# A new order list for every engine and for the transfer queue of a gated linear attention with an MLP behind it

## The chip, the cores and the metric

The kernel runs on one core of a Trainium2 chip. That core has a matrix engine (TensorE, PE in the profile, with its weight loads as PEld), a vector engine (VectorE, DVE), a scalar engine (ScalarE, ACT), a general engine (GpSimd, POOL), a sequencer that only issues transfers here (SyncE, SP), and 16 DMA engines that carry the transfers. The metric is the device time of one execution in microseconds, as the median of several executions; lower is better.

## The reference

Four batches of eight heads with 768 steps and a head width of 48 go through a gated linear attention, and its output (3072 tokens of 384 features) through a two-layer MLP with a leaky ReLU.

```
f = 1 / (1 + exp(-f_logit))
for t in range(S):
    state = f[:, :, t, :, None] * state + outer(k[:, :, t], v[:, :, t])
    y[:, :, t] = q[:, :, t] @ state
...
h = x @ w_in                      # 3072 x 384 by 384 x 2048
g = max(0.01 * h, h)
out = g @ w_out                   # 2048 x 384
```

## The kernel before

The recurrence is computed in chunks of 128 steps: decayed scores inside a chunk, a state carried between chunks. The work is cut into 12 units of 256 tokens. Units 0 to 3 are one batch each, with its first two chunks ("paired"); units 4 to 11 are one later chunk (c = 2 to 5) of two batches. Every unit goes through the same steps. The code keeps a function for each step, and the words below are the keys of the table `parts`:

- `Lf`, `Lk`, `Lq`, `Lv`: loads of the gate logits, k, q and v, all issued by SP (L161 for paired units, L165 for the others). The number at the end is the half (0 or 1), or 2 for both halves at once.
- `ge`, `gl`: exp and ln on ACT, giving the log of the gate; `cs`: its cumulative sum by matmuls on PE (L232 to L243); `dec`: exp of the sums on ACT.
- `k`, `q`: k and q times the decays (L263), on DVE (last number 0) or on POOL (last number 1); `v`: v to bf16 on POOL (L268 and after).
- the turning of k and q: for paired units on PE (`tk`, `tq`, L296) with copies out (`ck`, `cq`), for the others by a transposing DMA on SP's queue (`xk`, `xq`, L316).
- `sc`: scores on PE (L332, L339); `mk`: their mask on DVE (L349, L353); `mx`, `ms`: scores times v and the carried state (L370); `xt`: the result as the MLP's input; `pt`, `sf`, `sb`: the update of the state (PE L435 and L440, DVE, POOL).
- `up`: one of 8 groups of the first layer, 6 matmuls of 256 columns (L468); `pr`: leaky ReLU on ACT (L473); `dn`: a quarter of the second layer for 128 tokens, 4 matmuls of 384 columns (L480); `dh`: half of the columns of the last 128 tokens, all 16 matmuls (L496); `ob`, `st`: copy out of PSUM and store (L515 on SP).
- `WI`, `WO`: the weights in four blocks each, loaded by SP in fp32 (L170, L174) into the last two raw buffers, and turned to bf16 (`CI`, `CO`) in thirds on DVE, ACT or POOL.
- `F`: fills, matmuls of 512 columns on constant data whose result nobody reads; the number is their count.

Nothing is scheduled by the compiler. One string, `order`, lists all steps, with the engine where there is a choice, and after `@` the PSUM banks. The program walks this string and emits each step, so each engine's queue holds its steps in the string's order, SP's loads, transposes and stores among them. Every engine works through its own queue strictly in order and waits where data or a buffer is not ready.

```
    for word in order.split():
        word, _, at = word.partition("@")
        name, *numbers = word.split("_")
        parts[name](*[int(n) for n in numbers], *[int(n) for n in at.split(".") if n])
```

Buffers also set the order: six raw buffers for f and k and six for q and v (unit j uses number j modulo 6), three buffers for scaled k and q, two for the turned ones, three for the MLP's input and inner layer, four output tiles, eight PSUM banks.

Of the kernel before, what the change touches and what calls it, by code (L numbers as in the profile page):

```python
# [15 lines left out]
def kernel(  # L16
# [134 lines left out]
    def raw(j, x):  # L151
        return (raw_fk if x in "fk" else raw_qv)[j % NB][:, "fkqv".index(x) % 2]

    def by_pair(t):
        return t.rearrange("t a h d -> t (a h d)").rearrange("t (h s d) -> t h s d", s=2, d=D)

    def load(x):
        def go(j, a):
            if paired(j):
                h = slice(0, H) if a == 2 else slice(4 * a, 4 * a + 4)  # L160
                nc.sync.dma_start(out=by_pair(raw(j, x))[:, h].rearrange("t h s d -> t h (s d)"),  # L161
                                  in_=srcs[x][j, h, 0:2 * C, :].rearrange("h (t s) d -> t h (s d)", s=2))
            else:
                c, h = units[j]
                nc.sync.dma_start(out=raw(j, x)[:, a],  # L165
                                  in_=srcs[x][2 * h + a, :, c * C:(c + 1) * C, :].rearrange("h t d -> t h d"))
        return go
# [368 lines left out]
    pt_1_2@4.6 dec_0_0 k_0_0_1 ck_1_0_0 F_2@0 sc_1_0@5.7 ge_2_1 ge_2_0 q_0_0_1 sf_1_0 sc_0_1@0.3 mk_1_0_1 gl_2_1
    tk_0_0@2 mk_1_0_0 sb_1_0 F_1@4 cs_2_1@1 tq_0_0@4 mx_1_2@7.5 gl_2_0 ge_3_1 ck_0_0_0 v_0_0 cs_2_0@2 ge_3_0 gl_3_1
    dec_2_1 v_0_1 cq_0_0_0 mk_0_1_0 mk_0_1_1 xt_1_0_0 ms_1 zs_0_1 pt_0_2@4.0 sc_0_0@1.3 xt_1_1_1 gl_3_0 CI_3_2_1
    CI_3_0_2 sf_0_0 sb_0_0 CI_3_1_0 mk_0_0_1 cs_3_1@5 dec_3_1 dec_2_0 cs_3_0@7 k_2_0_1 mk_0_0_0 up_1_7@4 up_1_6@5
    q_2_0_1 pr_1_7 mx_0_2@3.1 pr_1_6 k_2_1_0 zv_2_1 q_2_1_0 ms_0 tk_2_0@2 tq_2_1@4 xt_0_1_1 xt_0_0_0 cq_2_1_0 sf_0_1  # L540
    dec_3_0 tk_2_1@5 ck_2_0_0 tq_2_0@3 CI_0_2_2 ck_2_1_0 CI_0_0_2 up_0_6@1 up_0_7@4 sf_1_1 v_2_0 cq_2_0_1 sc_2_0@7.0
    sc_2_1@3.2 v_2_1 mk_2_0_1 mk_2_1_1 mk_2_1_0 mk_2_0_0 CI_0_1_1 pr_0_7 up_0_0@5 up_1_1@4 CI_1_2_2 up_0_1@6 pr_0_1
    up_1_0@0 pt_2_2@2.3 pr_1_1 CI_1_1_1 mx_2_2@7.6 CI_1_0_0 pr_0_0 sf_2_0 q_3_0_0 xt_2_0_1 up_0_2@4 up_0_3@5 pr_1_0
    sb_2_0 ms_2 zs_3_0 k_3_0_0 sf_2_1 WO_0 CI_2_1_2 q_3_1_1 k_3_1_0 xt_2_1_1 up_1_2@2 up_1_3@7 CI_2_0_1 up_2_2@0
    up_2_7@6 WO_1 pr_0_2 CI_2_2_1 pr_2_2 pr_1_2 pr_0_6 pr_0_3 pr_1_3 up_2_5@4 up_0_4@0 WO_2 up_1_4@2 tq_3_1@1 pr_0_4
# [10 lines left out]
    cs_6_0@7 up_3_7@1 dn_2_0_1 dec_6_0 sb_2_1 k_5_2_1 q_5_2_0 up_3_6@0 xk_5 xq_5 Lv_4_1 v_5_2 Lk_6_0 Lq_6_0 ob_1_1_1
    st_1_1 Lq_6_1 dn_3_1_0@6 Lf_9_1 st_0_0 dn_3_1_1 gl_7_2 pr_3_7 pr_3_5 dn_3_0_1 sc_4_1@7.4 mk_4_1_0 pr_3_6
    sc_4_0@1.2 Lv_6_0 dn_3_0_2 Lf_8_0 v_4_2 dn_3_0_3 dn_3_1_2 dn_3_1_3 sc_5_0@0.7 mk_4_0_1 ob_3_0_1 mk_4_0_0 mk_4_1_1
    sc_5_1@2.1 pt_5_0@3 dn_2_0_2 cs_7_0@4 mk_5_0_1 mk_5_1_0 mk_5_1_1 dn_2_0_3 pt_4_1@7 mx_5_1@2 mk_5_0_0 sf_5_0
    dec_7_0 xt_5_1_1 mx_5_0@1 mx_4_1@4 mx_4_0@0 cs_6_1@3 xt_5_0_1 ob_3_1_1 dec_6_1 pt_4_0@2 up_5_3@1 up_5_4@6  # L560
    xt_4_1_1 up_5_5@3 Lf_8_1 Lf_9_0 sb_5_0 q_6_2_0 sf_4_1 Lq_8_1 xt_4_0_0 pr_5_5 pr_5_4 Lv_7_1 Lk_7_0 sb_4_1 up_5_6@4
    cs_7_1@7 k_6_2_0 Lk_7_1 sf_4_0 ob_2_0_0 dec_7_1 up_5_7@3 up_5_2@0 pr_5_6 sb_4_0 k_7_2_1 q_7_2_0 up_5_0@6 up_5_1@7
    pr_5_3 up_4_2@4 pr_5_0 up_4_6@2 up_4_1@1 up_4_4@5 pt_5_1@6 pr_5_1 up_4_0@7 xk_6 sf_5_1 pr_4_1 Lv_7_0 Lv_6_1 xq_6
    pr_5_7 up_4_7@1 pr_4_2 xk_7 v_7_2 pr_5_2 sb_5_1 xq_7 pr_4_0 ge_8_2 up_4_3@3 up_4_5@4 Lf_10_1 dn_5_0_0@6 pr_4_4
    dn_5_0_1 Lf_10_0 st_2_0 st_3_0 gl_8_2 pr_4_3 cs_8_0@0 pr_4_5 pr_4_7 pt_7_0@7 dn_4_0_0@5 dn_4_0_1 sf_7_0 pr_4_6
# [62 lines left out]
```

## Time and profile before

| | |
|---|---|
| three executions | 181.9, 183.21, 185.36 us; median 183.21 us |
| profiled execution | 180.78 us, of which the span from first to last instruction is 179.0 us |
| granted TensorE clock | 1.0 |
| busy in the span | PE 94%, PEld 73%, ACT 60%, DVE 46%, POOL 40% |
| DMA | 34.44 MB, mean 192 GB/s |

The profile is of one execution. "Idle before" is the time in which an engine stood still ahead of an instruction, with what ended that wait behind the arrow. In a timeline, a row merges equal instructions in a run; its first column is the start in microseconds, its second how long they took together, and a wait is shown in brackets. The chain of waits follows the last instruction back, from each step to what released it.

### The profile page before, as it was taken

The page shows a single profiled execution, that of the slowest core. Times are in us where ns is not written, and L with a number is a line of the kernel's source. Part 1 is how long each engine was busy: PE and PEld are TensorE (multiplying, and loading weights), DVE is VectorE, ACT ScalarE, POOL GpSimd, SP SyncE. Part 2 cuts the span into 40 slices and gives each one's busy share as a digit, 9 for nine tenths or more (in the row PEclk, how much of TensorE's full clock was granted, in tenths as well). Part 3 has the DMA queues.
Part 4 walks back from the last instruction along what each step waited for, and adds up shares of the span by engine and source line. Part 5 has one row for each costly group of instructions (what it writes and reads, how often), then busy time and mean ns, then how long its engine had stood idle before and what let it go on. Part 6 is the DMA issues. An engine that isn't in the chain of part 4 may idle for free.

```text
span 179.0 us, 5543 instructions
## 1 busy us (share of the span) xinstructions
PE 167.6 (94%) x2302; PEld 131.0 (73%) x2302; DVE 82.5 (46%) x172; ACT 108.1 (60%) x234; POOL 72.3 (40%) x143
## 2 busy tenths in 40 slices
...
GB/s 149 302 319 346 299 355 291 270 405 275 189 221 188 205 231 190 236 167 218 153 190 267 201 193 211 231 155 249 210 169 245 2 4 0 48 44 0 88 4 176
DMA packets 105961, 34.44 MB, mean 192 GB/s; under 512 B 100688, under 2 KB 103888, under 8 KB 105936
## 3 DMA queue, kind: packets, MB, share of 16 engines
...
q8 instruction: 18, 0.29, 0.7%
...
## 4 chain that ended last, share of the span: by engine, by line
PE 70%; DMA 12%; SPq 8%; issue 3%; DVE 3%; POOL 2%; ACT 0%; POOLq 0%; DVEq 0%
PE ps L468 31%; PE ps L480 27%; DMA raw_qv<-in_v_dram 7%; SPq L161 5%; PE ps L370 5%; DMA qT<-qh 5%; PE ps L339 2%; SPq L316 2%; POOL vb L268 1%; PE ps L240 1%; PE ps L440 1%; PE ps L296 1%; DVE wm L349 1%; PE ps L435 1%; DVE qh L263 1%
## 5 line engine op out<-in xcount | busy, mean ns | idle before, releaser
L473 ACT ACTIVATE gT<-ps 128x512 bf16<-128x512 f32 x96 | 52.7, 614 | 31.1 <-PE ps L468 28.9
L468 PE MATMUL ps<-xT,w_in 128*128 128x256 bf16 x576 | 69.7, 273 | 0.1
L480 PE MATMUL ps<-w_out,gT 128*128 128x384 bf16 x368 | 67.0, 326 | 0.0
L468 PEld LDWEIGHTS <-w_in 128*128 128x128 bf16 x576 | 61.7, 114 | 3.1 <-POOL w_in L184 0.2
L480 PEld LDWEIGHTS <-gT 128*128 128x128 bf16 x368 | 34.8, 98 | 19.4
L353 DVE TENSOR_TENSOR wm<-ps,ut 128x512 bf16<-128x512 f32 x32 | 20.1, 684 | 15.8 <-PE ps L339 15.6
L491 DVE COPY osb<-ps 128x384 f32<-128x384 f32 x13 | 7.2, 557 | 29.6 <-PE ps L480 28.7
L460 POOL CAST sb<-sf 64x192 bf16<-64x192 f32 x40 | 17.0, 425 | 4.5 <-DVE sf L450 2.4
L263 POOL TENSOR_TENSOR qh<-raw_qv,at 128x384 bf16<-128x384 f32 (+1 forms) x7 | 9.6, 1364 | 22.7 <-DMA raw_fk<-in_k_dram 11.8
L268 POOL CAST vb<-raw_qv 128x384 bf16<-128x384 f32 (+1 forms) x16 | 10.6, 663 | 16.1 <-DMA raw_qv<-in_v_dram 16.0
L452 DVE TENSOR_TENSOR sf<-sf,ps 64x192 f32<-64x192 f32 x32 | 11.2, 349 | 12.3 <-PE ps L440 10.6
L251 ACT ACTIVATE em<-ps 128x384 bf16<-128x384 f32 x24 | 12.0, 500 | 7.5 <-PE ps L240 3.9
L457 POOL TENSOR_TENSOR sf<-sf,end 128x192 f32<-128x192 f32 x16 | 8.8, 550 | 15.8 <-DVE sf L452 13.7
L422 ACT CAST xT<-ps 128x384 bf16<-128x384 f32 x16 | 7.9, 517 | 10.1 <-PE ps L370 9.0
L211 ACT ACTIVATE e<-raw_fk 128x384 f32<-128x384 f32 (+1 forms) x16 | 10.8, 692 | 3.1 <-DMA raw_fk<-in_f_logit_dram 3.1
L252 ACT ACTIVATE at<-ps 128x384 bf16<-128x384 f32 x24 | 12.1, 504 | 0.0
L263 POOL TENSOR_TENSOR kh<-raw_fk,em 128x768 bf16<-128x768 f32 (+1 forms) x7 | 10.7, 1541 | 3.2 <-DMA raw_fk<-in_k_dram 2.3
L263 DVE TENSOR_TENSOR qh<-raw_qv,at 128x768 bf16<-128x768 f32 (+1 forms) x9 | 8.4, 935 | 5.9 <-ACT at L252 4.1
L489 ACT COPY osb<-ps 128x384 f32<-128x384 f32 x10 | 4.9, 491 | 10.1 <-PE ps L480 6.1
L223 ACT ACTIVATE lf<-e 128x384 bf16<-128x384 f32 (+1 forms) x16 | 10.9, 693 | 0.1
L349 DVE TENSOR_TENSOR wm<-ps,pair_mask 128x512 bf16<-128x512 f32 x16 | 10.2, 684 | 1.2 <-PE ps L332 1.0
L263 DVE TENSOR_TENSOR kh<-raw_fk,em 128x384 bf16<-128x384 f32 (+1 forms) x9 | 7.2, 801 | 4.4 <-ACT at L252 2.8
...
## 6 DMA issues: line engine op xcount, KB each, us to landing
...
```

Source lines behind the costliest of these rows:

```text
L223: nc.scalar.activation(dst, src, AF.Ln, bias=1.0)
L251: nc.scalar.activation(ems[j % 2][:, a], t[:, 0:H * D], AF.Exp, scale=1.0)
L252: nc.scalar.activation(ats[j % 2][:, a], t[:, 0:H * D], AF.Exp, scale=-1.0)
L263: eng.tensor_mul(heads(j, to[j % NR], a)[:, :, :, 0:D], raw_heads(j, x, a), decays(j, by, a))
L268: nc.gpsimd.tensor_copy(out=heads(j, vb, a), in_=raw_heads(j, "v", a))
L349: nc.vector.tensor_mul(w.rearrange("t (s p) n -> t s p n", s=2), src.rearrange("t (s p n) -> t s p n", s=2, p=2), pair_mask[:, :, None, :] ...
L353: nc.vector.tensor_mul(w, src.rearrange("t (p n) -> t p n", p=P2), ut[:, None, :].to_broadcast([128, P2, 128]))
L452: nc.vector.tensor_add(sf[rows], sf[rows], new)
L460: nc.gpsimd.tensor_copy(out=sb[rows, :, y * D:y * D + D], in_=sf[rows])
L468: nc.tensor.matmul(pm[:, i, :], w_in_of(ff, kk), xTs[j % 3][:, kk].rearrange("t a s -> t (a s)"), start=(kk == 0), stop=(kk == NK - 1))
L473: nc.scalar.activation(gTs[j % 3][:, 2 * g:2 * g + 2, :], pm, AF.Prelu, alpha=0.01)
L480: nc.tensor.matmul(po, gTs[j % 3][:, ff, 128 * a:128 * a + 128], w_out_b[quarter][:, ff % 4, :], start=(ff == 0), stop=(ff == NF - 1))
```

## The change

The string `order` is replaced as a whole. The loader gets a third argument that could put a load on ACT's queue; no word of the new string passes it, so all loads, transposes and stores stay on SP's queue. All other functions are the same, one line further down (L268 is now L269). The counts of loads, transposes, matmuls and stores are the same but for the fills: 21 in six places instead of 14 in five (7, 5, 2, 2, 3 and 2 in place of 7, 1, 3, 2 and 1). All of them stand ahead of the first `up`, but for the last two of the new list, which stand behind its second.

Some steps change engine. Of the 16 copies of turned k and q, ACT has 9 instead of 3 and DVE 7 instead of 13; of the 16 scalings of k, POOL has 9 instead of 7, and of those of q 5 instead of 7; POOL writes the pair mask instead of DVE.

On SP's queue the start is in another order. The names raw_fk and raw_qv are the raw buffers, 64 and 70 those of unit 0, 65 and 71 of unit 1, and so on; `128x4x96` is half of a paired unit's operand, `128x8x96` a whole one. Before, the rows from the third on are:

```order
L161 DMA raw_qv_70<-in_q_dram 128x4x96
L161 DMA raw_fk_65<-in_k_dram 128x8x96
L161 DMA raw_qv_71<-in_q_dram 128x8x96
L161 DMA raw_fk_64<-in_k_dram 128x4x96
L161 DMA raw_fk_64<-in_f_logit_dram 128x4x96
L161 DMA raw_qv_71<-in_v_dram 128x8x96
L161 DMA raw_fk_66<-in_f_logit_dram 128x8x96
L161 DMA raw_fk_64<-in_k_dram 128x4x96
L161 DMA raw_qv_70<-in_q_dram 128x4x96
L161 DMA raw_fk_67<-in_f_logit_dram 128x8x96
L161 DMA raw_qv_70<-in_v_dram 128x4x96 x2
L170 DMA raw_qv_75<-in_moe_w_in_dram 128x3x512
```

Ahead of them stand the gate logits of unit 1 (whole) and the first half of unit 0's. In the changed list two halves of unit 0's gate logits come first, and then:

```order
L162 DMA raw_fk_65<-in_f_logit_dram 128x8x96
L162 DMA raw_fk_64<-in_k_dram 128x4x96
L162 DMA raw_qv_70<-in_v_dram 128x4x96
L162 DMA raw_qv_70<-in_q_dram 128x4x96
L162 DMA raw_qv_70<-in_v_dram 128x4x96
L162 DMA raw_fk_64<-in_k_dram 128x4x96
L162 DMA raw_fk_66<-in_f_logit_dram 128x8x96
L162 DMA raw_qv_70<-in_q_dram 128x4x96
L162 DMA raw_qv_71<-in_q_dram 128x8x96
L162 DMA raw_fk_65<-in_k_dram 128x8x96
L162 DMA raw_qv_71<-in_v_dram 128x8x96
L171 DMA raw_qv_74<-in_moe_w_in_dram 128x3x512
```

Unit 0 is loaded ahead of unit 1, and the first weights stand behind 18 half operands instead of 20: the gate logits of unit 3 now follow them.

On POOL's queue, in the middle of the program, the steps of units 4 to 6 are mixed otherwise. Here kh and qh are scaled k and q, vb and v the bf16 copies of v, sf and sb the state. Before:

```order
L263 TENSOR_TENSOR qh_85<-raw_qv_74,at_89 128x16x48
L457 TENSOR_TENSOR sf_115<-sf_115,end_93 128x192
L460 CAST sb_1_122<-sf_115 64x4x48 x2
L263 TENSOR_TENSOR kh_83<-raw_fk_69,em_88 128x16x48
L268 CAST vb_97<-raw_qv_75 128x768
L277 CAST v_100<-raw_qv_75 128x8x2x16
L268 CAST vb_96<-raw_qv_74 128x768
L277 CAST v_99<-raw_qv_74 128x8x2x16
```

After:

```order
L264 TENSOR_TENSOR kh_82<-raw_fk_68,em_87 128x16x48
L269 CAST vb_96<-raw_qv_74 128x768
L278 CAST v_99<-raw_qv_74 128x8x2x16
L264 TENSOR_TENSOR qh_84<-raw_qv_70,at_89 128x16x48
L264 TENSOR_TENSOR qh_86<-raw_qv_75,at_90 128x16x48
L264 TENSOR_TENSOR kh_81<-raw_fk_64,em_87 128x16x48
L264 TENSOR_TENSOR kh_83<-raw_fk_69,em_88 128x16x48
L458 TENSOR_TENSOR sf_114<-sf_114,end_91 128x192
```

Four scalings, q of unit 6, q of unit 5, k of unit 6 and k of unit 5, now stand on POOL one behind the other; before, only k of unit 5 was on POOL and the other three on DVE. Unit 6 is now turned and scored before unit 5.

The diff, cut to its core; of the string the lines in which the loads of v and the transposes stand that the prediction speaks of:

```diff
     def load(x):
-        def go(j, a):
+        def go(j, a, e=0):
+            queue = nc.scalar if e else nc.sync
             if paired(j):
                 h = slice(0, H) if a == 2 else slice(4 * a, 4 * a + 4)
-                nc.sync.dma_start(out=by_pair(raw(j, x))[:, h].rearrange("t h s d -> t h (s d)"),
+                queue.dma_start(out=by_pair(raw(j, x))[:, h].rearrange("t h s d -> t h (s d)"),
...
-    up_7_7@0 dn_5_1_3 sb_7_1 k_9_2_1 xk_8 st_4_1 dec_11_0 pr_6_2 pr_7_5 dec_10_1 Lv_8_0 v_8_2 ob_5_1_0 dn_7_1_1
-    Lq_11_1 Lk_11_0 sc_8_1@1.6 Lq_10_0 xk_9 sc_8_0@2.3 mk_8_1_0 dn_7_1_2 pt_8_1@4 sb_6_1 mk_8_0_0 xq_9 dn_6_0_0@1
...
+    up_4_4@6 sf_4_0 pr_4_1 pr_4_4 pt_4_1@5 st_0_0 xq_5 k_6_2_1 dn_3_1_1 Lf_7_0 up_4_6@3 xk_6 xq_6 sf_4_1 ob_2_0_1
+    k_5_2_1 up_4_3@7 dn_3_1_2 dn_3_1_3 pr_4_0 pr_4_3 dn_3_0_3 Lv_5_0 dn_4_0_0@6 sc_6_1@5.4 sc_6_0@2.7 ob_3_0_0 Lv_6_1
+    up_4_5@1 mk_6_1_0 Lf_8_1 st_2_1 sb_4_1 xk_5 ge_7_2 gl_7_2 pr_4_6 Lv_5_1 dn_4_1_0@3 mk_6_0_0 Lk_7_1 Lk_8_1 Lq_7_1
+    v_6_2 sb_4_0 pr_4_5 mk_6_0_1 mk_6_1_1 ob_3_1_0 Lf_8_0 Lf_10_0 sb_3_1 dn_4_0_1 dn_4_1_1 pt_6_1@5 st_2_0 Lv_7_0
```

More of the change, by code (lines that the diff above doesn't have):

```diff
@@ L164, in go @@
                 c, h = units[j]
-                nc.sync.dma_start(out=raw(j, x)[:, a],
+                queue.dma_start(out=raw(j, x)[:, a],
                                   in_=srcs[x][2 * h + a, :, c * C:(c + 1) * C, :].rearrange("h t d -> t h d"))
@@ L536 @@
[L536 to L545, printed above, removed]
@@ L556 @@
[L556 to L565, printed above, removed]
@@ L576 @@
-    Lk_10_1 Lq_10_1 st_4_0 pr_7_7 pr_6_3 dn_6_0_1 pt_8_0@0 dn_6_1_0@5 mk_8_0_1 st_5_1 up_6_6@2 dn_6_1_1 Lk_10_0
-    pr_6_6 sf_8_1 mk_8_1_1 v_9_2 sf_8_0 dn_6_1_2 dn_6_0_2 cs_10_0@3 Lq_11_0 Lv_11_1 sc_9_0@4.6 sc_9_1@0.2 dn_7_1_3
-    mk_9_0_1 mk_9_1_0 cs_11_1@6 st_5_0 Lv_11_0 dn_6_1_3 mk_9_0_0 ob_7_1_0 dec_10_0 pt_9_0@3 mk_9_1_1 dn_6_0_3 sb_8_0
-    mx_8_1@0 dec_11_1 q_11_2_1 k_10_2_1 mx_9_1@4 mx_9_0@6 xt_9_1_1 sf_9_0 ob_6_0_0 xq_11 mx_8_0@7 xt_8_0_0 q_10_2_0
-    xt_9_0_1 dn_7_0_0@2 st_6_0 pt_9_1@3 xt_8_1_0 up_9_0@4 sf_9_1 dn_7_0_1 up_9_1@1 up_8_4@6 pr_9_0 xq_10 up_9_5@7
@@ new lines @@
+    ge_9_2 pr_6_3 up_6_6@0 sb_6_0 q_8_2_0 k_8_2_0 gl_9_2 pr_5_7 dn_6_0_0@2 up_5_5@4 dn_6_1_0@3 xk_7 pr_5_2 up_6_7@6
+    dn_6_1_1 dn_5_0_0@5 pr_5_5 dn_6_1_2 xq_8 dn_6_0_1 cs_9_0@1 xk_8 dn_5_0_1 dn_6_0_2 ge_10_2 pr_6_6 pr_6_7 dec_9_0
+    cs_9_1@7 Lv_8_0 Lv_8_1 sc_7_0@4.0 sc_7_1@6.1 v_8_2 Lf_11_1 dn_6_0_3 dn_5_0_2 dn_6_1_3 ob_6_1_1 mk_7_1_0 mk_7_1_1
+    dn_5_1_0@6 mk_7_0_1 mk_7_0_0 sc_8_1@1.0 sc_8_0@4.3 st_3_0 st_4_0 Lv_9_1 Lk_10_0 Lq_9_1 Lk_9_1 dn_5_1_1 mk_8_1_0
+    mk_8_1_1 pt_7_1@1 mk_8_0_1 dn_5_1_2 sf_7_1 dn_5_0_3 mx_7_1@0 mk_8_0_0 mx_8_1@3 mx_7_0@1 mx_8_0@4 dn_5_1_3 Lv_10_1
@@ new lines @@
+    gl_10_2 xt_7_1_0 xt_7_0_0 ob_6_0_1 up_7_3@2 xt_8_1_1 Lq_9_0 Lk_9_0 pr_7_3 pt_7_0@0 up_7_7@3 cs_10_1@1 xt_8_0_1
+    up_7_0@2 dec_9_1 up_8_0@4 up_7_1@7 Lk_10_1 Lq_10_1 sf_7_0 up_7_4@0 Lk_11_1 dec_10_1 Lq_10_0 Lv_9_0 Lq_11_1 pr_7_0
+    pr_8_0 sb_7_0 pt_8_0@1 cs_10_0@2 ob_5_1_0 pr_7_7 up_8_6@6 sf_8_0 q_9_2_0 up_7_2@4 up_7_5@3 ge_11_2 k_9_2_1 sb_8_0
+    pr_8_6 pr_7_2 gl_11_2 st_6_0 up_8_3@1 xq_9 up_8_7@6 pr_7_5 pr_7_1 dec_10_0 pr_7_4 up_8_4@4 up_8_1@3 up_7_6@7
+    pt_8_1@2 up_8_2@0 pr_8_1 ob_5_0_0 k_10_2_0 q_10_2_0 xk_9 dn_8_0_0@5 Lk_11_0 pr_8_7 pr_8_4 dn_7_1_0@3 pr_7_6
```

83 lines of the change are left out of this document (48 added, 35 removed).

## The prediction

> **What bounds the kernel now.** I read the page first: span, busy engines, chain.
>
> ```profile
> span 179.0 us, 5543 instructions
> PE 167.6 (94%) x2302; PEld 131.0 (73%) x2302; DVE 82.5 (46%) x172; ACT 108.1 (60%) x234; POOL 72.3 (40%) x143
> PE 70%; DMA 12%; SPq 8%; issue 3%; DVE 3%; POOL 2%; ACT 0%; POOLq 0%; DVEq 0%
> ```
>
> PE is busy for 94% of the span and makes 70% of the chain that ends last. The change leaves PE's work as it is, fills aside, so it can only alter when PE starts in earnest, how often it waits, and what follows its last matmul. The timeline of PE shows four waits after the start that are longer than a pipeline's gap:
>
> ```profile
> 89.25 0.33 PE L440 MATMUL ps<-vb,kh 128*128 128x96 bf16 x4 [0.91 <-POOL vb L268]
> 93.04 0.40 PE L339 MATMUL ps<-qT,kT 48*128 48x128 bf16 x8 [0.30 <-DMA qT<-qh]
> 117.26 0.33 PE L440 MATMUL ps<-vb,kh 128*128 128x96 bf16 x4 [0.96 <-POOL vb L268]
> 123.39 0.62 PE L339 MATMUL ps<-qT,kT 48*128 48x128 bf16 x16 [0.91 <-DMA qT<-qh]
> ```
>
> Together 3.1 us: twice for a v that landed late, twice for a transposing DMA. Afterwards there is nothing to gain; by stages, the columns being the stretch, its length, the busy time of PE, PEld, DVE, ACT and POOL, the clock, the DMA share and GB/s:
>
> ```profile
> 140.00:150.00 10.00, 10.00 (x185) 8.45 (x184) 3.91 (x7) 5.30 (x11) 0.00 (x0) 1.00 0.01 2
> ```
>
> What is left is the start, where data arrive more slowly than PE could use them.
>
> **The start.** Timelines of ACT and POOL, the chain of waits, and the timeline of PE:
>
> ```profile
> 4.04 0.52 ACT L211 ACTIVATE e<-raw_fk 128x384 f32<-128x384 f32 x1 [2.02 <-DMA raw_fk<-in_f_logit_dram]
> 18.86 0.62 ACT L182 CAST w_in<-raw_qv 128x512 bf16<-128x512 f32 x1 [0.69 <-DMA raw_qv<-in_moe_w_in_dram]
> ```
>
> ```profile
> 16.47 0.50 POOL L268 CAST vb<-raw_qv 128x384 bf16<-128x384 f32 x1 [0.87 <-DMA raw_qv<-in_v_dram]
> 17.28 0.50 POOL L268 CAST vb<-raw_qv 128x384 bf16<-128x384 f32 x1
> ```
>
> ```profile
> 10.71 5.64 DMA raw_qv<-in_v_dram
> ```
>
> ```profile
> 18.46 0.26 PE L232 MATMUL ps<-lf,bu 128*128 128x192 bf16 x1
> ...
> 18.90 0.24 PE L232 MATMUL ps<-lf,bu 128*128 128x192 bf16 x1
> ...
> 19.56 1.68 PE L468 MATMUL ps<-xT,w_in 128*128 128x256 bf16 x12
> ...
> 22.21 0.35 PE L370 MATMUL ps<-qT,sb 128*32 128x128 bf16 x12
> 22.50 0.40 PE L296 MATMUL ps<-ident,kh 128*128 128x128 bf16 x4
> ...
> 23.64 0.39 PE L296 MATMUL ps<-ident,kh 128*128 128x128 bf16 x4
> ...
> 24.13 1.47 PE L468 MATMUL ps<-xT,w_in 128*128 128x256 bf16 x12
> 25.54 0.66 PE L332 MATMUL ps<-qT,kT 48*64 48x128 bf16 x32
> 26.13 2.81 PE L468 MATMUL ps<-xT,w_in 128*128 128x256 bf16 x24
> 28.87 0.51 PE L435 MATMUL ps<-vb,kh 64*128 64x96 bf16 x16
> 29.32 0.30 PE L370 MATMUL ps<-wm,vb 64*32 64x128 bf16 x16
> ...
> 30.06 1.50 PE L468 MATMUL ps<-xT,w_in 128*128 128x256 bf16 x12
> ```
>
> The first gate logits, two half operands, are used at 4.04 us. The load of v that the chain shows lands at 10.71 + 5.64 = 16.35 us; counted on SP's queue it ends with the 19th half. That is 12.3 us for 17 halves, 0.72 each. The first weights stand behind 20 halves in the old list and behind 18 in the new, so they land about 1.4 us earlier, at 17.4 instead of 18.8 us. The first `up` came 0.7 us after ACT could start its cast (18.86 to 19.56 us), which gives 18.1 us.
>
> The new list wants something else first: both halves of unit 1's v, which come with the 18th half, 4.04 + 16 x 0.72 = 15.6 us. POOL needs 0.81 us for each (16.47 to 17.28), so 17.2 us; then the state of unit 1 (0.45, from 28.87 to 29.32) and a cumulative sum (0.44, from 18.46 to 18.90). That also gives 18.1; with a gap, 18.2 us.
>
> As a common milestone I take the end of unit 2's state matmuls, 29.32 us before. From the first `up` to it, both lists hold eight `up`, one mix with its carried part, four turns, two scores and this state. The new list has two cumulative sums of unit 3 besides, which the old one did before its first `up`. By rows:
>
> ```profile
> 78.74 4.63 PE ps L468 x42
> ...
> 97.56 1.74 PE ps L370 x112
> ```
>
> ```profile
> 43.82 5.88 PE ps L480 x36
> ```
>
> In these chain rows 42 matmuls are seven `up`, so 0.66 each; nine `dn` take 5.88, so 0.65 each. The stretch is then 8 x 0.66 + mix 0.74 (29.32 to 30.06) + carried part 0.29 (22.21 to 22.50) + two pairs of turns at 0.49 (23.64 to 24.13) + scores 0.59 (25.54 to 26.13) + 0.45 = 8.33 us without a wait. It took 29.32 - 19.56 = 9.76, so 1.43 went into waits. The new list has 8.33 + 0.88 = 9.2: the milestone comes at 27.4 us without any wait, at 28.8 with the same 1.43. The gain lies between 0.5 and 1.9 us; I take the middle, **1.2**, since the later weights arrive no earlier (24 halves and one block stand ahead of the second block in both lists) and will still make PE wait somewhat.
>
> **The fills.** Timeline of PE:
>
> ```profile
> 2.02 3.13 PE L133 MATMUL ps<-filler 128*128 128x512 bf16 x7 [2.02 <-DVE filler L92]
> ...
> 9.18 0.81 PE L133 MATMUL ps<-filler 128*128 128x512 bf16 x3
> ```
>
> The first seven take 0.45 us each. The three at 9.18 overlap: with the 0.38 us that a single fill takes here, they start 0.21 us apart. Seven more are 7 x 0.21 = 1.5 us of PE. I cost them at nothing: what hides them is the waiting for unit 0's and unit 1's loads. Were that cover gone, the 1.5 us would be paid.
>
> **The middle.** Counted in the two strings by the work of PE between a transfer's word and the first matmul that needs it: before, `Lv_8_0` has two `dn` and two scores until `pt_8_1` (1.9 us), `xq_9` 4.9 us until `sc_9_0`; these are two of the four waits. The new list gives unit 8's and 7's v over 12 us, but has narrow places of its own: `xq_6` (one `up`, four `dn`, 3.3 us), `Lv_6_1` (one `up`, three `dn`, 2.6 us), `xk_5` (3.4 us), `xq_10` (3.6 us) and `xq_11` (1.3 us). Distance in the list is not time on SP's queue, so I bound each place by nothing and by the longest wait above, 0.96 us: 0 to 4.8 us, against 3.1 before. I take a little over half, 2.7 us, so a gain of **0.4**; ends: a gain of 3.1, a loss of 1.7.
>
> Moved copies and scalings load ACT, DVE and POOL otherwise, but these have 60, 46 and 40% busy time; I cost them at nothing except in the one place that the last rival names. The end of both lists (four stores, two halved second layers) is alike: nothing.
>
> **Sum.** 180.78 - 1.2 - 0.4 = 179.2 us for a profiled execution like this one. That execution lies 2.43 us below the median of the runs, 183.21, so the median forecast is 183.21 - 1.6 = **181.6 us**.
>
> **Rivals.**
>
> *Everything fits.* The full 1.9 us at the start and all 3.1 us of waits: 183.21 - 5.0 = 178.2 us. For it: the narrow v loads are gone. Against it: five new narrow places. Chance 0.22.
>
> *The gain is only moved.* PE reaches the milestone earlier, but transfers don't come sooner, and it waits in the middle for what it won: 183.2 us. For it: all four waits above end with a transfer or with the v that it brought, and the total of the transfers is the same. Chance 0.18.
>
> *POOL's four scalings hold SP's queue.* In the new list q of 6, q of 5, k of 6 and k of 5 follow one another on POOL, behind the conversion of unit 4's v; `xq_5`, `xk_6` and `xq_6` wait for them on SP, and all later loads stand behind those. By shapes, on POOL's and SP's timelines, and in the list of DMA issues:
>
> ```profile
> L263 POOL TENSOR_TENSOR kh<-raw_fk,em 128x768 bf16<-128x768 f32 x5 | 8.9, 1790 | 2.4 <-DMA raw_fk<-in_k_dram 2.3
> ...
> L263 POOL TENSOR_TENSOR qh<-raw_qv,at 128x768 bf16<-128x768 f32 x3 | 4.9, 1648 | 17.6 <-DMA raw_fk<-in_k_dram 11.8 <-DMA raw_qv<-in_q_dram 5.7
> ```
>
> ```profile
> 71.67 0.83 POOL L268 CAST vb<-raw_qv 128x768 bf16<-128x768 f32 x1 [6.40 <-DMA raw_qv<-in_v_dram]
> ```
>
> ```profile
> 40.39 4.41 SPq L165 DMA_DIRECT2D raw_fk<-in_f_logit_dram  x4
> ...
> 61.98 1.26 SPq L316 DMA_TRANSPOSE qT<-qh  x1
> ...
> 67.70 0.58 SPq L165 DMA_DIRECT2D raw_qv<-in_v_dram  x1
> ```
>
> ```profile
> qT<-qh SPq DMA_TRANSPOSE x8, 3.4
> ```
>
> The four take 2 x 1.65 + 2 x 1.79 = 6.9 us, the conversion of v some 1.2 (0.83 and its second part). Before, this v was used at 71.67 us, and POOL waited 6.4 us for it; it was the 57th transfer, 26 behind the one issued at 40.39, so 27.31 / 26 = 1.05 us per transfer. Now it is the 48th: 71.7 - 9 x 1.05 = 62.2 us. Then `xq_6` lands at 62.2 + 1.2 + 6.9 + 1.3 + 3.4 = 75.0. PE gets there at 28.1 plus 30 `up` (19.8), 33 `dn` (21.5), paired small work (4.1 by the rows above) and twelve small groups of later units (at most 0.44 by the L370 row of four mixes, some 3.4 together): 76.9 us. So 1.9 us are in hand; each microsecond beyond is a loss. If the gain in SP's order is only half there, v lands 4.7 us later and PE waits 2.8 us: 184.4. If it is all gone, 7.6 us: 189.2 us. Chance 0.14, half of it beyond 2%.
>
> *A cold array.* The fills at 2.02 us ran at half the pace of those at 9.18. If the new start, with more waiting, let PE fall back to that pace until the first `up`, its useful work there (six cumulative sums, eight turns, four scores, a mix with its carried part and two states, 7.7 us by the rows above) would take 15.4 us where 13.0 lie between the end of the first fills (2.02 + 3.13) and 18.2: 2.4 us more, 184.0 us. The trace shows the slow pace only ahead of the first useful matmul. The Trainium skill (TensorE: Matmul & The Clock Gate, Part 1: The HAM clock gate, and Part 4: PE-mode transpose) states that an idle window of about 3.4 us brings back half the clock and that transposes by matmul don't count as busy in the same way; by that rule the turns alone would not keep it warm, and no run here has shown it yet. Chance 0.04.
>
> **How the numbers follow.** The forecast has the rest, 0.42. A measurement of this kernel can tell about 2% (3.7 us) from no change: below 179.5 is faster, above 186.9 slower. Faster: most of "everything fits" and the lower edge of the forecast, 0.26. Slower: half of POOL's case, and paid fills (1.5) together with the worse end of the middle (1.7), 0.12. Within: 0.62. The three executions lie from 181.9 to 185.36 us, so a median moves by about 1 us by itself. The range runs from 178.0 (just under "everything fits") to 185.8 us (the middle's worse end, paid fills and half of POOL's case in part), which leaves out less than 2 in 10.
>
> **What would show it.** The first `up` at 18.2 and the milestone at 27.4 to 28.8 us on PE's timeline prove the start; the waits of L440 for vb and of L339 for qT and kT (now L441 and L340) prove the middle, with a sum under 4.8 us. The issue of `xq_6` after about 72 us, and idle PE ahead of unit 6's scores, would be the POOL case. Wrong is the whole if PE idles in the stretch after 140 us, where I see no cause for it.

## The result and the profile after

The changed kernel takes 178.9 us (median of four executions, 178.42 to 179.98). The kernel before took 182.56 us on the same chip (181.71 to 185.36). The ratio is 0.985 [0.980, 0.990], a gain of 1.5% or about 2.8 us; medians and ranges here are of all executions, ratios leave out the disturbed ones, in which the time or the clock stands out. The profiled execution took 178.9 us where before's took 180.78, and the span fell by 1.9 us, from 179.0 to 177.1. Before's profiled execution is shorter than any of the four above, so its profile shows a good execution of the old list, not a typical one.

The page of the changed kernel, first its span and busy engines, then the shares of the chain that ended last:

```profile
span 177.1 us, 5553 instructions
PE 168.5 (95%) x2309; PEld 131.8 (74%) x2309; DVE 79.4 (45%) x160; ACT 111.1 (63%) x239; POOL 71.4 (40%) x150
PE 79%; SPq 7%; DMA 5%; ACT 2%; DVE 2%; issue 2%; POOL 1%; POOLq 0%; DVEq 0%; ACTq 0%
```

PE is as busy as before. On the chain its share rose from 70 to 79%, and that of transfers fell from 12 to 5%. All waits of PE in the changed kernel, by what it waited for, with total, count and longest:

```profile
PE ps L133 <- DVE filler L92: 2.0, 1, 2.0
PE ps L297 <- POOL qh L264: 1.1, 2, 0.9
PE ps L297 <- DVE qh L264: 1.1, 1, 1.1
PE ps L133 <- DVE wm L350: 0.8, 1, 0.8
PE ps L469 <- DVE wm L350: 0.3, 1, 0.3
PE ps L469 <- ACT w_in L183: 0.2, 1, 0.2
```

Every one of them lies ahead of 28 us. The four waits of before for v and for turned q (L440 and L339, 3.1 us) have no counterpart: L441 and L340 are not in the list. The start, however, did not get shorter in this profile. Timelines of PE and of POOL:

```profile
16.25 0.81 PE L133 MATMUL ps<-filler 128*128 128x512 bf16 x3 [0.80 <-DVE wm L350]
...
20.18 1.50 PE L469 MATMUL ps<-xT,w_in 128*128 128x256 bf16 x12 [0.22 <-ACT w_in L183]
...
22.70 0.61 PE L133 MATMUL ps<-filler 128*128 128x512 bf16 x2
...
30.48 0.31 PE L371 MATMUL ps<-wm,vb 64*32 64x128 bf16 x16
```

```profile
18.86 0.61 POOL L185 CAST w_in<-raw_qv 128x512 bf16<-128x512 f32 x1 [0.57 <-DMA raw_qv<-in_moe_w_in_dram]
```

The first `up` came at 20.18 us (19.56 before), and the milestone, the end of unit 2's state matmuls, at 30.48 us (29.32 before): 1.2 us later. From there to the end of the span the changed kernel needs 177.1 - 30.48 = 146.6 us and before 179.0 - 29.32 = 149.7. The 3.1 us between them are the four waits, to the tenth. So in these two executions the span's gain of 1.9 us is 3.1 won in the middle less 1.2 lost at the start.

How the transfers lie to the end, from the same kind of table by stages as in the prediction, and from SP's timeline, both of the changed kernel:

```profile
120.00:140.00 20.00, 20.00 (x234) 15.49 (x231) 11.16 (x19) 12.16 (x25) 9.82 (x14) 1.00 1.09 199
140.00:150.00 10.00, 10.00 (x194) 8.64 (x192) 5.73 (x11) 4.99 (x10) 3.99 (x9) 1.00 0.52 124
```

```profile
138.64 2.02 SPq L317 DMA_TRANSPOSE qT<-qh  x1
...
141.33 0.42 SPq L166 DMA_DIRECT2D raw_qv<-in_v_dram  x1
```

The same places in SP's timeline of the kernel before, and its stage ahead of 140 us:

```profile
126.57 0.43 SPq L165 DMA_DIRECT2D raw_qv<-in_v_dram  x1
...
132.84 2.69 SPq L316 DMA_TRANSPOSE kT<-kh  x2
```

```profile
120.00:140.00 20.00, 19.09 (x281) 15.30 (x279) 10.36 (x20) 8.83 (x18) 12.57 (x20) 1.00 0.85 196
```

Before, SP issued the last v at 126.57 us and the last transposes from 132.84 us on, and after 140 us 2 GB/s moved. In the changed kernel they are issued at 141.33 and 138.64 us, and 124 GB/s move between 140 and 150 us. Yet PE is busy for all of 120 to 150 us. Up to 140 us both move nearly the same 200 GB/s: the stream is not faster, its end is asked for later.

### The profile page after: what moved, and what is told of

Its sections match the earlier page's. It is cut to its first block, busy times and chain, and to the rows that moved or that the text cites. A ratio compares the mean times of both kernels' runs of the same rounds, so it can differ in the third digit from the quotient of the medians.

```text
span 177.1 us, 5553 instructions
## 1 busy us (share of the span) xinstructions
PE 168.5 (95%) x2309; PEld 131.8 (74%) x2309; DVE 79.4 (45%) x160; ACT 111.1 (63%) x239; POOL 71.4 (40%) x150
## 4 chain that ended last, share of the span: by engine, by line
PE 79%; SPq 7%; DMA 5%; ACT 2%; DVE 2%; issue 2%; POOL 1%; POOLq 0%; DVEq 0%; ACTq 0%
PE ps L469 35%; PE ps L481 29%; PE ps L371 6%; SPq L162 4%; SPq L317 3%; DMA raw_qv<-in_q_dram 3%; DMA raw_qv<-in_v_dram 3%; PE ps L340 2%; DVE wm L350 2%; PE ps L497 1%; PE ps L241 1%; PE ps L441 1%; ACT gT L474 1%; PE ps L133 1%; PE ps L333 1%
## 5 line engine op out<-in xcount | busy, mean ns | idle before, releaser
L474 ACT ACTIVATE gT<-ps 128x512 bf16<-128x512 f32 x96 | 53.3, 626 | 24.9 <-PE ps L469 24.8
L269 POOL CAST vb<-raw_qv 128x384 bf16<-128x384 f32 (+1 forms) x16 | 10.6, 663 | 31.5 <-DMA raw_qv<-in_v_dram 30.2
L492 DVE COPY osb<-ps 128x384 f32<-128x384 f32 x12 | 6.5, 553 | 32.0 <-PE ps L481 31.9
L264 POOL TENSOR_TENSOR kh<-raw_fk,em 128x768 bf16<-128x768 f32 (+1 forms) x9 | 12.5, 1402 | 14.7 <-DMA raw_fk<-in_k_dram 8.0
L461 POOL CAST sb<-sf 64x192 bf16<-64x192 f32 x40 | 15.7, 392 | 4.4 <-DVE sf L451 2.3
L264 DVE TENSOR_TENSOR qh<-raw_qv,at 128x768 bf16<-128x768 f32 (+1 forms) x11 | 9.2, 851 | 9.8 <-DMA raw_qv<-in_q_dram 9.7
L423 ACT CAST xT<-ps 128x384 bf16<-128x384 f32 x16 | 8.4, 534 | 6.2 <-PE ps L371 6.1
L350 DVE TENSOR_TENSOR wm<-ps,pair_mask 128x512 bf16<-128x512 f32 x16 | 10.3, 683 | 1.4 <-PE ps L333 0.9
L133 PE MATMUL ps<-filler 128*128 128x512 bf16 x21 | 7.0, 463 | 2.8 <-DVE filler L92 2.0
L264 DVE TENSOR_TENSOR kh<-raw_fk,em 128x384 bf16<-128x384 f32 (+1 forms) x7 | 5.8, 829 | 6.4 <-ACT em L252 6.2
```

The lines of the kernel that those rows point to most:

```text
L264: eng.tensor_mul(heads(j, to[j % NR], a)[:, :, :, 0:D], raw_heads(j, x, a), decays(j, by, a))
L350: nc.vector.tensor_mul(w.rearrange("t (s p) n -> t s p n", s=2), src.rearrange("t (s p n) -> t s p n", s=2, p=2), pair_mask[:, :, None, :] ...
L461: nc.gpsimd.tensor_copy(out=sb[rows, :, y * D:y * D + D], in_=sf[rows])
L474: nc.scalar.activation(gTs[j % 3][:, 2 * g:2 * g + 2, :], pm, AF.Prelu, alpha=0.01)
```

## The experiments

Three questions stood. Is it the place of single late transfers in SP's queue that cost before its waits? Or does the new list leave the whole stream of transfers more reserve? And what do the fills do at the start? A term used below: the rest, which is the span less the milestone less all PE waits after it. Each job ran on one chip together with the kernel before; ratios are to it. The chips were not the same, and before's median went from 181.89 to 184.83 us with them, so times are compared within a job.

### Fewer fills: the last five left out

```
-mk_0_0_0 mk_0_0_1 F_3@4 tk_1_0@6 sc_1_1@5.0
+mk_0_0_0 mk_0_0_1 tk_1_0@6 sc_1_1@5.0
...
-v_2_0 v_2_1 F_2@7 cs_3_0@0 q_2_0_0
+v_2_0 v_2_1 cs_3_0@0 q_2_0_0
```

> The changed kernel without two of its six fill places: the three fills in bank 4 and the two in bank 7 (the last five fills). Theory (these fills lie on the chain): the chain of the changed kernel holds 0.81 and 0.54 us of fills that start only when the turn of k of unit 1 and the cumulative sum of unit 3 could start; without them the first up-matmul comes some 0.6 us earlier, the end of unit 2's state matmuls some 1.1 us earlier (29.4 instead of 30.5 us), and the time is about 1 us below the changed kernel, a ratio to before of 0.979. Rival (hidden, as the prediction had it): PE waits for data there anyway, no change, ratio 0.985. Second rival (the array gets cold): matmuls after the missing fills start at half pace, the milestone comes later than 30.5 us, ratio 0.99 or more.

Measured: 180.14 us (179.66 to 181.36), ratio 0.977 [0.970, 0.985]. PE's timeline:

```profile
19.70 1.57 PE L469 MATMUL ps<-xT,w_in 128*128 128x256 bf16 x12 [0.60 <-ACT w_in L183]
...
84.71 0.62 PE L340 MATMUL ps<-qT,kT 48*128 48x128 bf16 x16 [0.69 <-DMA kT<-kh]
...
139.64 0.62 PE L340 MATMUL ps<-qT,kT 48*128 48x128 bf16 x16 [0.64 <-DMA qT<-qh]
144.61 0.62 PE L340 MATMUL ps<-qT,kT 48*128 48x128 bf16 x16 [0.81 <-DMA qT<-qh]
```

The first `up` is 0.5 us earlier and the milestone 0.7 (29.76 us), but 2.7 us of waits stand in the middle of this execution. The three rows are scores that wait for a turned k or q (units 5, 10 and 11), and the fourth wait is one of 0.58 us for ACT. The three are the narrow places `xk_5`, `xq_10` and `xq_11` that the prediction named. The new list, then, is not without narrow places; it has little to spare there.

### Before with three v loads moved ahead, with the turn of unit 9 moved ahead, and with both

The first edit changes places of loads in before's list: both late v of unit 7 and 6 with both gate logits of unit 9, and `Lv_8_0` with `Lv_10_1`.

```
-Lq_6_1 dn_3_1_0@6 Lf_9_1 st_0_0
+Lq_6_1 dn_3_1_0@6 Lv_7_0 st_0_0
...
-up_5_5@3 Lf_8_1 Lf_9_0 sb_5_0
+up_5_5@3 Lf_8_1 Lv_6_1 sb_5_0
...
-sf_5_1 pr_4_1 Lv_7_0 Lv_6_1 xq_6
+sf_5_1 pr_4_1 Lf_9_1 Lf_9_0 xq_6
...
-up_7_1@5 dec_9_1 Lv_10_1 up_7_5@2
+up_7_1@5 dec_9_1 Lv_8_0 up_7_5@2
...
-pr_7_5 dec_10_1 Lv_8_0 v_8_2
+pr_7_5 dec_10_1 Lv_10_1 v_8_2
```

> The kernel before, with three loads of v exchanged with loads that are needed later (Lv_7_0 and Lv_6_1 with Lf_9_1 and Lf_9_0, Lv_8_0 with Lv_10_1); all else as before. Theory (place in the transfer queue): the two waits of PE for vb, 0.91 and 0.96 us, go, and the span falls by up to 1.9 us, ratio 0.990. Rival (the wait moves on): the transfers' total is the same, PE meets the next late transfer and waits there, ratio 1.000.

Measured: 185.26 us (183.01 to 186.66), ratio 1.000 [0.994, 1.006]. The profiled execution is the longest of the ten (186.66 us). PE's timeline has 8.0 us of waits after the milestone, among them four for a turned q or k, the longest of 2.02 us, and one at the first of the two places that the edit was to mend, unit 7's v. Timelines of PE and of POOL:

```profile
92.78 0.33 PE L440 MATMUL ps<-vb,kh 128*128 128x96 bf16 x4 [1.62 <-POOL vb L268]
```

```profile
90.32 1.64 POOL L263 TENSOR_TENSOR kh<-raw_fk,em 128x768 bf16<-128x768 f32 x1 [4.85 <-DMA raw_fk<-in_k_dram]
91.90 0.82 POOL L268 CAST vb<-raw_qv 128x768 bf16<-128x768 f32 x1
```

POOL did not wait for this v any more. It converted it late because a scaling of k stands ahead of it in POOL's queue, and that waited 4.85 us for its load.

The second edit moves both turns of unit 9 ahead of three loads:

```
-dn_7_1_1 Lq_11_1 Lk_11_0 sc_8_1@1.6 Lq_10_0 xk_9 sc_8_0@2.3
+dn_7_1_1 xk_9 xq_9 Lq_11_1 Lk_11_0 sc_8_1@1.6 Lq_10_0 sc_8_0@2.3
...
-sb_6_1 mk_8_0_0 xq_9 dn_6_0_0@1
+sb_6_1 mk_8_0_0 dn_6_0_0@1
```

> The kernel before, with the two transposes of unit 9 moved ahead of three loads (q and k of unit 11, q of unit 10) in the transfer queue. Theory (place in the queue): the transposes land about 3 us earlier, the wait of 0.91 us ahead of unit 9's scores goes, ratio 0.995. Rival (the wait moves on): PE waits for unit 10's or 11's data later, ratio 1.000.

Measured: 183.79 us (182.55 to 186.01), ratio 0.999 [0.994, 1.004]. The profiled execution is again the longest (186.01 us). Unit 9's scores don't wait any more. PE's timeline, of which the first row has a wait that before's profile did not show, and the others stand at the two v that it did:

```profile
72.74 0.62 PE L339 MATMUL ps<-qT,kT 48*128 48x128 bf16 x16 [1.28 <-DMA qT<-qh]
92.39 0.33 PE L440 MATMUL ps<-vb,kh 128*128 128x96 bf16 x4 [2.30 <-POOL vb L268]
...
122.49 0.33 PE L440 MATMUL ps<-vb,kh 128*128 128x96 bf16 x4 [1.57 <-POOL vb L268]
```

The wait at 72.74 us, for unit 5's turned q, can't come from this edit, since the list is changed only behind it.

Both edits together:

> The kernel before with both edits, the three early loads of v and the two early transposes. Theory: three of the four waits go, 2.8 of 3.1 us; with the start of before unchanged the time falls by 2.8 us, ratio 0.985, as far as the changed kernel got. Rival (the wait moves on): 1.000. If the changed kernel's gain comes from elsewhere (its start, its engines), this one stays above 0.992.

Measured: 186.21 us (183.95 to 188.4), ratio 1.006 [1.000, 1.011]. PE's timeline:

```profile
72.62 0.63 PE L339 MATMUL ps<-qT,kT 48*128 48x128 bf16 x16 [1.94 <-DMA qT<-qh]
...
129.62 0.24 PE L370 MATMUL ps<-wm,vb 128*32 128x128 bf16 x4 [2.46 <-DVE wm L353]
142.10 0.84 PE L339 MATMUL ps<-qT,kT 48*128 48x128 bf16 x24 [1.97 <-DMA kT<-kh]
```

No wait for v is left, nor one for unit 9's q, but 6.5 us of others are, the longest at 129.62 and 142.10 us, later in the list than the places that were mended. The theory of single places falls by the three ratios: with these transfers moved ahead, PE waits in other places. That it is the transfers they were moved past that come late is likely, but not shown.

### Twelve stores less, in both lists

The stores of units 0 to 5 are left out, so those rows of the output stay unwritten; that is 12 x 192 KB of the stream. The same words go from the old and from the new list:

```
-q_4_2_1 Lv_5_0 st_1_0 pr_3_3 dn_1_1_3
+q_4_2_1 Lv_5_0 pr_3_3 dn_1_1_3
...
```

> The kernel before without the 12 stores of units 0 to 5 (those rows of the output are not written). Theory (the stream of transfers is the bound in the middle, and the old list leaves PE no reserve against it): some 0.55 us of the stream go with each store, 6.6 us in all, and PE's waits of 3 to 6 us go with them: ratio to before 0.97 to 0.985. Rival (the waits belong to single places in the queue, not to the stream's pace): two or three of them stay, ratio 0.99 or more.

> The changed kernel without the 12 stores of units 0 to 5 (those rows of the output are not written). Theory (the new list has the reserve): PE hardly waits in the middle, so it gains at most 1 to 2 us on the changed kernel, ratio to before 0.975 to 0.985, that is no faster than the old list without these stores by more than 1%. Rival (places, not pace): it gains nothing.

Measured, on a chip where before took 184.83 us: 180.6 us from the old list (179.36 to 181.59), ratio 0.982 [0.971, 0.993], and 178.47 from the new one (177.4 to 179.11), ratio 0.970 [0.960, 0.980]. The longest wait in PE's timeline of the old list without the stores:

```profile
72.81 0.62 PE L339 MATMUL ps<-qT,kT 48*128 48x128 bf16 x16 [1.14 <-DMA qT<-qh]
```

With no load moved at all, 1.8% of the time went, as the theory has it. In the profile the waits for v are gone, but three others with 2.5 us are left (the two not shown are 0.61 and 0.71 us), as its rival has it. So part of before's middle hangs on the stores. Whether by the bytes or because SP no longer stops for outputs that aren't ready, this run doesn't tell. The new list has no PE wait after 28 us here. It stays 2.1 us or 1.2% ahead of the old one without the stores, more than the 1% at most that was expected, so this part of its lead isn't a matter of the stores. Its 178.47 us lie close to the 178.9 and 179.4 us that it takes with all stores, though on other chips; the whole list was not run on this chip, so what the stores are worth to it isn't settled.

### Six loads twice

Six loads of gate logits (`Lf_8_0` to `Lf_10_1`) are issued twice in a row in each list; one of the places in the new one:

```
-mk_6_1_0 Lf_8_1 st_2_1 sb_4_1
+mk_6_1_0 Lf_8_1 Lf_8_1 st_2_1 sb_4_1
...
```

> The kernel before, with six loads of gate logits (units 8 to 10) issued twice in a row. Theory (stream): 6 x 0.9 = 5.4 us more of the stream, all of it behind a queue that PE already waits for: 4 to 5.4 us slower, ratio 1.022 to 1.03. Rival (places): the doubled loads lie in the slack of their units, ratio below 1.01.

> The changed kernel, with the same six loads issued twice. Theory (stream, with a reserve of some 3 us of PE's work): 1 to 3 us slower than the changed kernel, ratio to before 0.99 to 1.0, so less harm than the same loads do to the old list. Rival (both lists stand in the stream alike): 4 to 5.4 us slower, ratio 1.005 to 1.015.

Measured: 200.97 us (198.76 to 202.14) from the old list, ratio 1.087 [1.065, 1.109]; 197.72 (196.76 to 200.14) from the new one, 1.074 [1.061, 1.086]. The old list lost 16 us against before on that chip, and the new one is 18 to 19 above what it takes elsewhere. SP's waits, first of the old list so edited, then of the new:

```profile
SPq L165 <- DMA raw_fk<-in_f_logit_dram: 16.5, 6, 3.1
```

```profile
SPq L166 <- DMA raw_fk<-in_f_logit_dram: 17.5, 6, 3.4
```

The second load goes into the buffer that the first still fills, so SP stands still until the first has landed, six times 2.8 us and more. The experiment measured a stalled queue instead of a longer stream. It says nothing for or against the theory of reserve; both lists suffer alike.

### The new list once more, with the fills taken away in two steps, and with scalings on DVE

These ran in one job, on a chip where before took 181.89 us (179.72 to 183.35). The first is the changed kernel as it is:

> The changed kernel once more, on the same chip as the next three, and a second profile of it. If the middle is where its gain lies, the time from the end of unit 2's state matmuls to the end of the span stays near 146.6 us plus whatever PE waits in between, and that milestone again comes later than the 29.3 us of before. Ratio to before 0.98 to 0.99.

Measured: 179.4 us (178.59 to 180.26), ratio 0.988 [0.983, 0.993]. The second leaves out the last five fills, as above:

> The changed kernel without the three fills in bank 4 and the two in bank 7, as in the first run of this edit, now beside the changed kernel on the same chip. Theory (these fills lie on the chain): 0.7 to 1.1 us below the changed kernel, ratio to before 0.005 lower. Rival (what is won at the start is waited for in the middle, since the transfers come no sooner): the same time as the changed kernel within 0.2%.

Measured: 178.18 us (177.65 to 180.11), ratio 0.983 [0.978, 0.989]. PE's timeline of the changed kernel, then that without the five fills:

```profile
30.59 0.31 PE L371 MATMUL ps<-wm,vb 64*32 64x128 bf16 x16
...
85.11 0.62 PE L340 MATMUL ps<-qT,kT 48*128 48x128 bf16 x16 [0.56 <-DMA kT<-kh]
```

```profile
29.77 0.30 PE L371 MATMUL ps<-wm,vb 64*32 64x128 bf16 x16
...
84.90 0.62 PE L340 MATMUL ps<-qT,kT 48*128 48x128 bf16 x16 [1.09 <-DMA kT<-kh]
```

Without them the milestone is 0.8 us earlier (30.59 to 29.77), and 0.5 of it goes to a longer wait at `xk_5`. It is the fastest version here, by 0.5% of ratio; the intervals overlap.

The third keeps only the first seven fills:

```
-q_0_1_0 v_0_0 F_5@3 tq_0_1@2 zs_0_1
+q_0_1_0 v_0_0 tq_0_1@2 zs_0_1
...
-tk_0_0@4 F_2@3 tq_0_0@2 Lk_1_2 F_2@5 cs_2_1@3
+tk_0_0@4 tq_0_0@2 Lk_1_2 cs_2_1@3
```

> The changed kernel with only the first seven fills. Theory (of the other fourteen only the last five lie on the chain): the same as with 16 fills. Rival (cold array): without fills the PE of the start idles up to 2 us at a time, falls back to the pace of the first fills, and the milestone comes 1 to 2 us later than with 16 fills.

Measured: 181.62 us (179.51 to 184.6), ratio 0.996 [0.991, 1.001]. Against the second that is 1.25% or 2.3 us lost. PE's timeline, and the stage by stretches with the clock in the third column from the end:

```profile
9.19 0.61 PE L297 MATMUL ps<-ident,qh 128*128 128x128 bf16 x4 [2.85 <-DVE qh L264]
9.59 0.37 PE L233 MATMUL ps<-lf,bu 128*128 128x192 bf16 x1
9.75 0.37 PE L234 MATMUL ps<-lf,bs 128*128 128x192 bf16 x1
...
21.41 0.35 PE L371 MATMUL ps<-qT,sb 128*32 128x128 bf16 x12 [2.48 <-issue]
...
23.15 2.47 PE L469 MATMUL ps<-xT,w_in 128*128 128x256 bf16 x12
...
34.41 0.30 PE L371 MATMUL ps<-wm,vb 64*32 64x128 bf16 x16
```

```profile
10.00:15.00 5.00, 5.00 (x71) 4.49 (x69) 3.36 (x10) 4.17 (x12) 3.89 (x7) 0.50 1.05 290
...
20.00:25.00 5.00, 3.59 (x45) 2.78 (x45) 2.10 (x6) 2.74 (x7) 1.74 (x4) 0.68 0.74 226
```

After a wait of 2.85 us the cumulative sums start 0.16 us apart, where rows of the changed kernel have 0.08, and the granted clock is 0.50 from 10 to 15 us, against 1.00 there with the fills. By unit 1's last scores that has cost 0.7 us: they start at 18.52 us, against 17.84 with 16 fills. Then PE stands still for 2.48 us, and the profile shows nothing that it waits for; behind that the clock falls again (0.68 in the mean from 20 to 25 us). So the first `up` comes 3.4 us later and the milestone 4.6, less the 1.1 that the other version waits at `xk_5`. More than half of that is a stop whose cause the profile doesn't show, and this is one of the longer executions (182.59 us). The nine fills do hold the clock: ten of the twelve executions without them have a mean clock of 0.991 or less, and none of the six with 16 fills. But the other two, with 0.998 and 0.997, took 180.57 and 181.19 us, where 16 fills took 177.65 to 180.11. That these fills are worth some 2 us is shown; how much of it is the clock is not.

The fourth puts `q_6`, `q_5` and `k_6` from POOL to DVE, to free POOL at the place of the last but one rival:

```
-dn_3_0_1 q_6_2_1 q_5_2_1 mx_4_1@7
+dn_3_0_1 q_6_2_0 q_5_2_0 mx_4_1@7
...
-st_0_0 xq_5 k_6_2_1 dn_3_1_1
+st_0_0 xq_5 k_6_2_0 dn_3_1_1
```

> The changed kernel with three of the four scalings that follow one another on POOL (q of unit 6, q of unit 5, k of unit 6) on DVE. Rival of the prediction (POOL's four scalings hold the transfer queue): the transposes of units 5 and 6 are issued some 3 us earlier, waits ahead of their scores go, and the time falls by 0.5 to 1 us. Theory (PE's reserve at that place covers it): no change, within 0.3% of the changed kernel; if DVE's other work is pushed back by 3 us, up to 1 us slower.

Measured: 180.2 us (179.33 to 181.55), ratio 0.993 [0.989, 0.998]: no gain, 0.5% behind the unchanged list. But the transposes did not come earlier: `xq_6` was issued at 75.76 us, against 74.85 in the changed kernel's profile. So the run doesn't tell what an earlier issue would be worth. One PE wait of 0.33 us came in at 72.53 us, for a copy of the MLP's input, which DVE did later.

### What the runs make of it together

| profile | milestone | PE waits after it | rest |
|---|---|---|---|
| before | 29.3 | 3.1 | 146.6 |
| before, v loads moved | 30.0 | 8.0 | 146.9 |
| before, turns moved | 29.2 | 6.2 | 148.8 |
| before, both | 28.9 | 6.5 | 148.5 |
| before, 12 stores less | 29.9 | 2.5 | 146.3 |
| before, six loads twice | 29.5 | 16.8 | 153.0 |
| changed | 30.5 | 0.0 | 146.6 |
| changed, again | 30.6 | 0.6 | 146.6 |
| last five fills out | 29.8 | 2.7 | 147.1 |
| last five fills out, again | 29.8 | 1.1 | 146.2 |
| seven fills | 34.4 | 0.0 | 146.4 |
| changed, 12 stores less | 29.6 | 0.0 | 146.0 |
| changed, six loads twice | 30.2 | 13.1 | 151.6 |
| scalings on DVE | 31.0 | 0.5 | 147.0 |

Sums of the rows in PE's timelines, in us. The rest is the same within 1.1 us in both lists, but for the two versions with unit 9's turns moved, where it is some 2 us more, and the two with loads issued twice, where it is 5 to 6.5 us more (their mean clock was 0.94 and 0.96). The stages of these two with the lowest clock, and one behind a wait of equal length, the clock again in the third column from the end; first the version with the turns moved, then with both edits:

```profile
92.00:96.00 4.00, 3.61 (x18) 1.93 (x18) 0.70 (x2) 1.14 (x4) 3.75 (x9) 0.67 0.96 182
```

```profile
72.00:76.00 4.00, 3.38 (x32) 2.07 (x32) 2.91 (x6) 0.54 (x2) 1.17 (x2) 0.64 1.14 228
129.00:133.00 4.00, 3.38 (x85) 2.76 (x85) 3.92 (x7) 1.47 (x3) 2.70 (x2) 1.00 0.74 164
```

Behind the waits of 2.30 us at 92.39 and of 1.94 us at 72.62 the clock fell for some 3 us, which costs about half of that again. Behind the 2.46 us at 129.62 it did not. So a wait of two microseconds can cost more than itself. It doesn't even take one: in before's list without the stores the clock fell at the start, from 10 to 13 us, where the longest wait since 5 us was one of 0.79 us and PE was busy for 53 to 69% of each microsecond from 6 to 10:

```profile
10.00:13.00 3.00, 3.00 (x32) 1.94 (x31) 2.55 (x5) 2.00 (x4) 2.42 (x8) 0.50 1.06 283
```

The clock also parts the two lists where no profile was kept. In 21 of 55 executions of the kernel before, those beside the experiments, its mean was 0.991 or less, and these are the longer ones (medians of 185.0 and 183.4 us with and without on one chip, 182.6 and 181.7 on another). In all 24 executions of the new list with its 21 fills, the loads issued twice aside, it was 0.996 or more. This is not what the gain rests on: on the chip of the last job the new list's 179.4 us are 1.2% below the 181.7 as well.

The edits also serve as repeats, since most of them leave the start of their list alone. In the six profiles of the old list's start the first `up` comes at 19.56 to 20.92 us and the milestone at 28.9 to 30.0; in the five of the new list with all its fills at 19.30 to 20.53 and 29.6 to 31.0. By their means the new list's first `up` is 0.3 us earlier and its milestone 0.9 us later; before's profile has the earliest first `up` of its list. It also lacks a wait of 1.1 to 2.0 us for unit 5's turned q, near 73 us, which all five others of the old list show, two of them with nothing added or moved ahead of that place. So the 3.1 us of waits in before's profile are rather too few for its list.

What differs is the milestone and the waits. Shown is, then, that the gain is the waits in the middle: 3.1 us before, 0 and 0.6 us in the two profiles of the changed kernel. With the edits, but without the loads issued twice, it is 2.5 to 8.0 us in the old list (the 8.0 and the 6.2 in executions that were the longest of ten) and 0 to 2.7 in the new one. Shown is also that moving these single transfers in the old list doesn't bring the gain, and that leaving out twelve stores brings part of it.

Which part of the new order does it stays open. The rows at 120 to 150 us speak for a later need of the last data at the same pace of transfers; the experiment that was to test reserve failed on the stalled queue, and nothing else isolated it.

## Why the prediction was right, and where not

**The number.** Forecast was 181.6 us with 178.0 to 185.8; 178.9 us was measured, within 2% of before. For the profiled execution the sum said -1.6 us and -1.9 came. That closeness is luck: both terms were off, in opposite directions. The median forecast is off by 2.7 us because it put the 2.43 us on top by which before's profiled execution lay below its median; the changed kernel's profiled execution is its median.

**The start: wrong.** The first step that failed is that the first weights land 1.4 us earlier because 18 instead of 20 halves stand ahead of them. POOL could begin with them at 18.86 us, the very time at which ACT could before. Up to v the count held in this profile: unit 1's v landed at 15.59 us by its issue and landing in the trace, where 15.6 was expected. But the weights took 3.2 us more, where the prediction had left 1.8, the time from the 20th half by its count (17.0 us) to the weights in before's profile. It had taken the old start's pace for the new one's. The stages from 10 to 20 us, of before and of the changed kernel, show that less moved (the last column, GB/s); up to 10 us the two are alike, with 236 and 233 GB/s:

```profile
10.00:20.00 10.00, 9.00 (x242) 6.80 (x243) 9.48 (x21) 8.37 (x22) 8.11 (x21) 1.00 1.12 326
```

```profile
10.00:20.00 10.00, 8.04 (x224) 5.55 (x221) 7.90 (x18) 8.59 (x21) 7.61 (x18) 1.00 0.98 282
```

These 44 GB/s over 10 us are 440 KB, more than the two halves of 192 KB that the new list has less ahead of the weights. Why less moved stays open, and part of it is chance: the six profiles of the old start have 299 to 326 GB/s there and first use the weights at 18.9 to 20.0 us, the five of the new one 282 to 308 GB/s and 18.4 to 19.3 us. By their means the weights come 0.5 us earlier, not 1.4.

The second failed step is that the first `up` follows the weights by 0.7 us. In this profile it followed by 1.3, since ACT's third of the cast stood behind its copies of unit 0's result (`xt`), and these behind PE's small work. The chain of waits of the changed kernel shows that PE work, with fills in it:

```profile
16.25 0.81 PE ps L133 x3
...
17.63 0.74 PE ps L371 x61
...
19.51 0.63 ACT w_in L183
```

From the first `up` to the milestone it took 10.3 us, within the 9.2 to 10.6 that the prediction allowed.

**The fills: half wrong.** "I cost them at nothing" holds for those ahead of the first loads, not for the last five. Three of them wait 0.80 us for the mask that holds their bank and then delay unit 1's turn, and two stand at 22.70 us ahead of unit 3's cumulative sums with nothing to hide them. Leaving these five out brought the milestone 0.8 us forward, near half of the 1.5 us that the prediction set as the price without cover.

**The middle: the mechanism right, the size wrong.** The waits were named with their transfers, and they went. The term was -0.4, of a span from -3.1 to +1.7; it measured -3.1, the end that was held for "everything fits". What failed is the choice of "a little over half" of the worst case for the five narrow places. Three of them do show waits, of 0.6 to 1.1 us each, in other executions, so they are narrow, but seldom all at once.

**The rivals.** "Everything fits" (178.2 us) comes nearest in time, though its half at the start fell. "The gain is only moved" fell by the runs: there was no gain at the start to move. What is moved are waits within the old list, when single transfers change place. POOL's four scalings: `xq_6` was indeed issued after 72 us (74.85), but unit 6's scores followed without a wait. POOL could take up unit 4's v at 66.42 us, not at the expected 62.2, about as late as in the case in which half of the gain in SP's order is lost; PE came late as well, at 79.62 us instead of 76.9, and so the reserve lasted. Taking three scalings from POOL doesn't settle it, since the transposes came no earlier by it. The sign chosen for this case, an issue after about 72 us, was too strict by some 3 us.

The rows, SP's and PE's timelines of the changed kernel:

```profile
74.85 1.24 SPq L317 DMA_TRANSPOSE qT<-qh  x1
```

```profile
79.62 0.62 PE L340 MATMUL ps<-qT,kT 48*128 48x128 bf16 x16
```

**The cold array: not here, but real.** The changed kernel's granted clock stayed at 1.0, though its first cumulative sums, from 4.97 us on, still start 0.16 us apart. With seven fills it fell to 0.50 from 10 to 15 us. That 2.3 us were lost where 2.4 had been worked out is luck: up to 18.5 us the slow pace cost 0.7 us, and the profile's largest loss is a stop with no cause shown. The Trainium skill (TensorE: Matmul & The Clock Gate, Part 1: The HAM clock gate) puts the idle window that brings this back at about 3.4 us, free-running; here the traces show the slow pace behind waits of 2.85, 2.48, 2.30, 1.94 and even 0.79 us, and the full pace behind others of 2.46, 2.02, 1.97 and 1.94. So the length of one wait doesn't decide it, and far shorter waits than the page's figure were enough.

**What would show it wrong.** PE does not idle after 140 us, as said.
